# Attention decode with a key and a value cache: a quarter of each value tile weighed on GpSimd, and wider matmuls elsewhere

## The chip, the core and the metric

The kernel runs on one core of a Trainium2 chip. The time is the device time of one execution, in microseconds (us); a median over several executions is given where there are several. A profile is one further execution recorded by the hardware profiler. Its span, from the first to the last recorded instruction, is a little shorter than the device time of the same execution.

Names of engines in the profile: PE is TensorE (matmuls), PEld its weight loads, DVE is VectorE, ACT is ScalarE, POOL is GpSimd, SP is SyncE, which here issues nearly all DMAs. L252 is line 252 of the kernel.

## What is computed

One decode step of a transformer block for a batch of 4, with one query token each, in fp32. The attention reads a key and a value cache of 4 x 32 heads x 4096 positions x 128 values; these two, 268 MB each, are nearly all the bytes there are.

```python
mod = (_silu(c) @ w_mod).reshape(B, 6, 1, -1)          # c: 4x512, w_mod: 512x3072
sa, ca, ga, sb, cb, gb = (mod[:, i] for i in range(6))
h = _layernorm(x) * (1 + ca) + sa
q = (h @ wq) per head                                   # wq: 512x4096
scores = einsum("bhqd,bhkd->bhqk", q, k_cache) * Dh ** -0.5
o = einsum("bhqk,bhkd->bhqd", softmax(scores), v_cache)
x = x + ga * (o @ wo)                                   # wo: 4096x512
h = _layernorm(x) * (1 + cb) + sb
x = x + gb * (_silu(h @ w1) @ w2)                       # w1: 512x1792, w2: 1792x512
```

## The kernel before

**Tiles and slots.** The 128 pairs of batch and head are taken four heads at a time: 32 tiles, numbered n, with n = 4t + b for head group t (0 to 7) and batch b (0 to 3). A key tile k(n) and a value tile v(n) are 128 partitions x 128 rows x 128 values each, 8 MB. A partition holds 128 consecutive positions of one head. All big tiles share three slots of SBUF (`kv`, 3 buffers), given out in the order w_mod, wq, k0, v0, k1, v1, and so on to k31, v31, wo, then w1 with w2. So v(n+1) goes where k(n) was and k(n+2) goes where v(n) was: the load of v(n+1) waits for the last read of k(n), and the load of k(n+2) for the last read of v(n). SP issues the loads in this order and stands still at each wait.

**One iteration n** (loop at L353; the order on each engine is the order of the program text, since the schedule is written by hand):

- `mult` (L252): the key tile times the query, in place. GpSimd takes rows 0 to 55 (NA = 56, 7168 elements per partition) with the query from SBUF (`qw`), DVE rows 56 to 127 (9216 elements) with the query from PSUM (`qb`). `make_qb(n + 1)` prepares the next query: ACT picks a row of `qn`, a matmul spreads it over the partitions, ACT copies it to SBUF.
- `red` (L257): DVE sums each row over its 128 values into a score, first its own 72 rows, then GpSimd's 56.
- `rowmax`, `bmax`, `negmax` (L261 to L273): the maximum for the softmax, through one PE transpose. `softexp` (L279): ACT's exp. Then GpSimd writes the probabilities into two zero-padded tiles of weights, `pz` (L281, two instructions of 256 elements).
- `pv` (L297): 32 matmuls, each 4 rows of v (512 columns), accumulating in the PSUM tile `po`; the profile counts two instructions for each. Two batches share one `po` tile.
- Every second iteration `gather` (L308, L314) picks the diagonal blocks out of `po` on DVE and sums them with four matmuls. At the first batch of the next head group, `spread` (L332 to L337) scales and transposes the result for the output product.

In the last iteration (n = 31) the key tile comes in two halves, and GpSimd takes 28 of the 64 rows of each.

**Ahead and behind.** `mods` (L183) makes the six modulation vectors and L221 the queries, while the first tiles land. After the loop `project` (L346) multiplies with wo, and the feed-forward follows (L415 to L442). `busy` (L411) issues matmuls whose result nobody reads. The load of w1 and w2 is issued when the last sums over k31 are done, since it goes into k31's slot.

Of the kernel before, what the change touches and what calls it, by code (L numbers as in the profile page):

```python
# [17 lines left out]
def kernel(  # L18
# [14 lines left out]
    P = 128  # L33
# [17 lines left out]
    NA = 56  # L51
    SCALE = 1.0 / math.sqrt(Dh)
# [54 lines left out]
    tmp = s0.take(P)  # L107
    csT, hT = s0.take(NK, W), s0.take(NK, W)
# [50 lines left out]
    for t in pz:  # L159
        nc.gpsimd.memset(t, 0.0)  # L160
    oz = const.tile([P, NT, R, B], F32, name="oz")
# [15 lines left out]
    def mods(dsts, i):  # L177
        p = psum([P, 4, P], "q", 2)
        for u in range(len(dsts)):
            for k in range(NK):  # L180
                for g in range(G):
                    o = (i + u) * D + g * P
                    nc.tensor.matmul(  # L183
                        p[W * g : W * (g + 1), u, :], csT[:, k, :], wmt[:, k, o : o + P],
                        start=k == 0, stop=k == NK - 1,
                    )
        for u, d in enumerate(dsts):
            nc.scalar.activation(
                d, p[:, u, :], AF.Copy,
                scale=0.25 if i + u == 5 else 0.5, bias=1.0 if i + u in (1, 4) else 0.0,  # L190
            )
# [48 lines left out]
    def make_qb(n):  # L240
        m = work.tile([P, Dh], F32, tag="lnu", name=f"qm{n}", bufs=1)
        nc.scalar.activation(m, qn, AF.Copy, scale=sel[:, n : n + 1])  # L242
        p = psum([P, Dh], "q", 2)
        nc.tensor.matmul(p, blk.rearrange("p i x -> p (i x)"), m, start=True, stop=True)  # L244
        qb[n] = p
        qw[n] = work.tile([P, Dh], F32, tag="qw", name=f"qw{n}")
        nc.scalar.activation(qw[n], p, AF.Copy)  # L247
# [27 lines left out]
    def softexp(n):  # L275
        t, b = divmod(n, B)
        if b == 0:
            rs[t] = work.tile([P, B], F32, tag="rs", name=f"rs{t}")
        nc.scalar.activation(sc[n], sc[n], AF.Exp, bias=nm[n], accum_out=rs[t][:, b : b + 1])  # L279
        for h in range(2):  # L280
            nc.gpsimd.tensor_mul(  # L281
                pz[h][:, : HG * W].rearrange("p (g x) -> p g x", g=HG)[:, :, E:].rearrange("p g (i j) -> p g i j", i=HP),
                sc[n][:, HG * JJ * h : HG * JJ * (h + 1)].rearrange("p (g j) -> p g j", j=JJ)
                .unsqueeze(2).to_broadcast([P, HG, HP, JJ]),
                hm.unsqueeze(1).unsqueeze(3).to_broadcast([P, HG, HP, JJ]),
            )

    def pv(n):
        t, b = divmod(n, B)
        q, a = divmod(b, 2)  # L290
        if a == 0:
            po[t, q] = psum([P, JJ * Dh], "po", 2)
        for j in range(NG):
            g = j % G
            h, u = divmod(j, HG)
            o = u * W + (1 - a) * E
            nc.tensor.matmul(  # L297
                po[t, q][W * g : W * (g + 1), :],
                pz[h][:, o : o + W],
                vt[n][:, JJ * j : JJ * (j + 1), :].rearrange("p j d -> p (j d)"),  # L300
                start=(a == 0 and j < G), stop=(a == 1 and j >= NG - G),
            )
# [3 lines left out]
    def gather(t, q):  # L306
        o = work.tile([P, JJ, Dh], F32, tag="o", name="o", bufs=1)
        nc.vector.tensor_mul(  # L308
            o, po[t, q].rearrange("p (j d) -> p j d", j=JJ), jm.unsqueeze(2).to_broadcast([P, JJ, Dh])
        )  # L310
        if q == 0:
            od[t] = psum([P, Dh], "od", 1)
        for j in range(JJ):
            nc.tensor.matmul(  # L314
                od[t], spick[:, 2 - 2 * q : 2 - 2 * q + P], o[:, j, :],
                start=(q == 0 and j == 0), stop=(q == 1 and j == JJ - 1),
            )
# [21 lines left out]
    accp = psum([P, P], "acc", 1)  # L339
    nc.vector.memset(accp, 0.0)  # L340

    def project(lo, hi):
        for t in range(lo, hi):
            for r in range(R):
                for g in range(G):
                    nc.tensor.matmul(  # L346
                        accp[W * g : W * g + B, :], oz[:, t, r, :], wot[:, t, r, g * P : (g + 1) * P],
                        start=(t == 0 and r == 0), stop=(t == NT - 1 and r == R - 1),
                    )
# [3 lines left out]
    for n in range(N):  # L353
# [13 lines left out]
        if n + 1 < N:  # L367
            mult(nc.gpsimd, qw, n, 0, NA)
            mult(nc.vector, qb, n, NA, NJ)
            make_qb(n + 1)  # L370
            red(n, NA, NJ)
        else:
            for lo in (0, NJ // 2):
                mid, hi = lo + NA // 2, lo + NJ // 2
                mult(nc.gpsimd, qw, n, lo, mid)
                mult(nc.vector, qb, n, mid, hi)
                red(n, mid, hi)
            red(n, NJ // 2, NJ // 2 + NA // 2)
# [4 lines left out]
        red(n, 0, NA if n + 1 < N else NA // 2)  # L383
# [14 lines left out]
        if b == B - 1:  # L398
            norm(t)
        pv(n)  # L400
# [5 lines left out]

    idle = psum([P, P], "q", 2)
# [5 lines left out]
    x1, hg, y = (s2.take(P) for _ in range(3))  # L413
    h2T, hid, th, hidT = s2.take(NK, W), s2.take(FG), s2.take(FG), s2.take(NI, W)
    nc.vector.tensor_mul(x1, ga, accp)  # L415
    nc.vector.tensor_add(x1, x1, xg)
    busy(4)
    layernorm_mod(hg, x1, sb, cb1)
    transposed(h2T, hg, NK)
    busy(5)  # L420
# [7 lines left out]
    busy(6)  # L428
# [39 lines left out]
```

## Time and profile before

| what | before |
|---|---|
| device time, median of 3 (lowest to highest) | 1323.45 us (1323.44 to 1323.78) |
| device time of the profiled execution | 1323.81 us |
| its span | 1321.9 us |
| busy: DVE, POOL, PE, ACT | 923.3, 533.5, 398.0, 44.7 us |
| busy share of the 16 DMA engines by queue q1 | 99.4% |
| moved, mean rate | 567.76 MB, 430 GB/s |

In the profile's second part, the 40 slices of the span, the DMA row reads 9 (90% or more) in all slices but the last, which has 8. In the parts that group instructions, a row gives the line, engine, operation, output and inputs, how often, then the busy time in us and the mean of one instruction in ns, then the idle time of the engine just ahead of these instructions and what ended it. In a timeline the first number is the start, the second the duration; a bracket gives the idle time before.

### The profile page before, as it was taken

What the parts mean: (1) busy time and instruction counts of PE and PEld (TensorE: products, weight loads), DVE (VectorE), ACT (ScalarE), POOL (GpSimd) and SP (SyncE); (2) the same over time, 40 slices, a digit from 0 to 9 for tenths busy, and PEclk for the clock granted to TensorE, in tenths of its full rate; (3) what the DMA queues carried; (4) which work ended last, traced back from release to release, by engine and by line L of the source; (5) the groups of instructions that cost most, each with busy time, mean ns of one, the idle gap of its engine ahead of it and who ended that gap; (6) DMA issues with size and microseconds to landing.
All of it is one profiled execution on the core that took longest, in us unless ns stands there. A gap on an engine that the chain in (4) does not pass through costs nothing.

```text
span 1321.9 us, 7059 instructions
## 1 busy us (share of the span) xinstructions
PE 398.0 (30%) x2998; PEld 145.4 (11%) x2998; DVE 923.3 (70%) x335; ACT 44.7 (3%) x146; POOL 533.5 (40%) x111
## 2 busy tenths in 40 slices
PE   3321223323123333212333321323332132333146
PEld 2100001101010010101001010100100010010014
DVE  1267877766887666788667678776668876676971
ACT  1100000000000000000000000000000000000000
POOL 1234455433445533354543334454334445433540
PEclk9765566665566666566666656666655666665569
DMA  9999999999999999999999999999999999999998
GB/s 414 441 418 439 442 419 438 439 424 431 441 430 429 437 436 427 436 436 429 435 433 435 428 435 438 426 435 440 423 435 444 418 437 444 419 437 439 420 422 330
DMA packets 12287, 567.76 MB, mean 430 GB/s; under 512 B 1440, under 2 KB 1504, under 8 KB 2272
## 3 DMA queue, kind: packets, MB, share of 16 engines
q1 hardware_dynamic: 12048, 567.29, 99.4%
q8 instruction: 23, 0.38, 0.1%
q14 instruction: 8, 0.07, 0.0%
q0 software_dynamic: 128, 0.01, 0.0%
q10 hardware_dynamic: 80, 0.02, 0.0%
HBM read 567.30 MB, written 0.01 MB: 429 GB/s over the span
## 4 chain that ended last, share of the span: by engine, by line
DMA 32%; issue 31%; POOL 25%; PE 7%; DVE 4%; POOLq 0%; SPq 0%; DVEq 0%
DMA k<-in_A_k_cache_dram 26%; POOL k L252 24%; PE po L297 6%; DMA w<-in_B_w_dram 3%; DMA wq<-in_A_wq_dram 3%; DVE sc L257 3%; DVE k L252 1%; POOL pz L281 1%; PE q L221 1%; PE mx L231 0%; POOLq L281 0%; DVE o L308 0%; PE po L434 0%; PE mx L265 0%; SPq L123 0%
## 5 line engine op out<-in xcount | busy, mean ns | idle before, releaser
L252 POOL TENSOR_TENSOR k<-k,qw 128x7168 f32<-128x7168 f32 (+1 forms) x33 | 491.4, 14893 | 290.1 <-DMA k<-in_A_k_cache_dram 264.7
L257 DVE TENSOR_REDUCE sc<-k 128x72 f32<-128x9216 f32 (+2 forms) x66 | 554.4, 8422 | 1.1
L252 DVE TENSOR_TENSOR k<-k,q 128x9216 f32<-128x9216 f32 (+1 forms) x33 | 312.3, 9463 | 309.3 <-DMA k<-in_A_k_cache_dram 300.1
L297 PE MATMUL po<-v,pz 128*32 128x512 f32 x2048 | 292.1, 735 | 48.6 <-POOL pz L281 47.9
L281 POOL TENSOR_TENSOR pz<-sc,hm 128x256 f32<-128x256 f32 x64 | 37.9, 612 | 458.1 <-ACT sc L279 445.7
L265 PE MATMUL mx<-ident,rm 128*128 128x128 f32 x32 | 14.5, 453 | 531.2 <-DVE rm L261 531.2
L314 PE MATMUL od<-o,spick 128*128 128x128 f32 x128 | 32.3, 431 | 293.4 <-DVE o L308 293.4
L297 PEld LDWEIGHTS po<-v,pz 128*32 128x32 f32 x2048 | 71.2, 132 | 248.2 <-issue 191.9
L265 PEld LDWEIGHTS mx<-ident,rm 128*128 128x128 f32 x32 | 5.8, 181 | 538.8 <-issue 332.1
L314 PEld LDWEIGHTS od<-o,spick 128*128 128x128 f32 x128 | 27.7, 319 | 296.5 <-DVE o L308 296.3
L279 ACT ACTIVATE sc<-sc,nm 128x128 f32<-128x128 f32 x32 | 12.8, 401 | 891.9 <-DVE nm L273 891.9
L270 DVE TENSOR_REDUCE hx<-mx 128x4 f32<-128x128 f32 x32 | 9.3, 291 | 19.7 <-PE mx L265 19.7
L247 ACT ACTIVATE qw<-q 128x128 f32<-128x128 f32 x32 | 8.9, 277 | 302.9 <-PE q L244 302.9
L308 DVE TENSOR_TENSOR o<-po,jm 128x512 f32<-128x512 f32 x16 | 10.9, 680 | 8.4 <-PE po L297 8.4
L244 PE MATMUL q<-qm,blk 128*128 128x128 f32 x64 | 15.6, 326 | 1.5 <-ACT qm L242 1.5
L183 PE MATMUL q<-wm 128*32 128x128 f32 x192 | 9.2, 375 | 20.3 <-DVE wm L170 20.3
L244 PEld LDWEIGHTS q<-qm,blk 128*128 128x128 f32 x64 | 9.5, 188 | 27.0 <-issue 25.1
L242 ACT ACTIVATE qm<-qn,sel 128x128 f32<-128x128 f32 x32 | 12.4, 387 | 0.9 <-DMA xg<-in_A_x_dram 0.9
L221 PE MATMUL q<-wq,wm 128*32 128x512 f32 x64 | 9.3, 748 | 7.4 <-DMA wq<-in_A_wq_dram 7.4
L183 PEld LDWEIGHTS q<-wm 128*32 128x32 f32 x192 | 7.8, 153 | 21.0 <-DVE wm L170 20.3
L261 DVE TENSOR_REDUCE rm<-sc 128x1 f32<-128x128 f32 x32 | 9.1, 284 | 0.9
L167 DVE SCALAR_TENSOR_TENSOR wm<-wm 128x128 f32<-128x128 f32 x1 | 0.3, 291 | 12.3 <-ACT wm L166 12.3
(79 smaller groups left out, 104.2 us busy)
## 6 DMA issues: line engine op xcount, KB each, us to landing
k<-in_A_k_cache_dram SPq DMA_DIRECT2D x2, 4096.0 KB
wm<-in_w_mod_dram SPq DMA_DIRECT2D x1, 6144.0 KB
wo<-in_A_wo_dram SPq DMA_DIRECT2D x1, 4096.0 KB
wo<-in_A_wo_dram SPq DMA_DIRECT2D x1, 2048.0 KB
wo<-in_A_wo_dram SPq DMA_DIRECT2D x2, 1024.0 KB, 35.2
w<-in_B_w_dram SPq DMA_DIRECT2D x2, 1024.0 KB
w<-in_B_w_dram SPq DMA_DIRECT2D x1, 1792.0 KB
w<-in_B_w_dram SPq DMA_DIRECT2D x2, 896.0 KB
```

The costliest lines, as they stand in the source:

```text
L183: nc.tensor.matmul(p[W * g : W * (g + 1), u, :], csT[:, k, :], wmt[:, k, o : o + P], start=k == 0, stop=k == NK - 1,)
L221: nc.tensor.matmul(pq[i][W * g : W * (g + 1), :], hT[:, k, :], wqt[:, k, ch * CW : (ch + 1) * CW], start=k == 0, stop=k == NK - 1,)
L242: nc.scalar.activation(m, qn, AF.Copy, scale=sel[:, n : n + 1])
L244: nc.tensor.matmul(p, blk.rearrange("p i x -> p (i x)"), m, start=True, stop=True)
L252: eng.tensor_mul(kt[n][:, lo:hi, :], kt[n][:, lo:hi, :], src[n].unsqueeze(1).to_broadcast([P, hi - lo, Dh]))
L257: nc.vector.tensor_reduce(sc[n][:, lo:hi], kt[n][:, lo:hi, :], axis=AX.X, op=ALU.add)
L265: nc.tensor.transpose(p, nm[n].to_broadcast([P, P]), ident)
L279: nc.scalar.activation(sc[n], sc[n], AF.Exp, bias=nm[n], accum_out=rs[t][:, b : b + 1])
L281: nc.gpsimd.tensor_mul(pz[h][:, : HG * W].rearrange("p (g x) -> p g x", g=HG)[:, :, E:].rearrange("p g (i j) -> p g i j", i=HP), sc[n][:, ...
L297: nc.tensor.matmul(po[t, q][W * g : W * (g + 1), :], pz[h][:, o : o + W], vt[n][:, JJ * j : JJ * (j + 1), :].rearrange("p j d -> p (j d)") ...
L308: nc.vector.tensor_mul(o, po[t, q].rearrange("p (j d) -> p j d", j=JJ), jm.unsqueeze(2).to_broadcast([P, JJ, Dh]))
L314: nc.tensor.matmul(od[t], spick[:, 2 - 2 * q : 2 - 2 * q + P], o[:, j, :], start=(q == 0 and j == 0), stop=(q == 1 and j == JJ - 1),)
```

## The change

- **Values.** In iterations 0 to 30, rows 0 to 31 of v(n) leave the matmuls. GpSimd multiplies them in place with their probabilities (`vmult`, 4096 elements per partition) and adds rows 16 to 31 onto rows 0 to 15 (`fold`, 2048). One iteration later (`vsum(n - 1)`, behind DVE's `mult` of k(n)) DVE adds rows 8 to 15 onto 0 to 7 and 4 to 7 onto 0 to 3 (1024 and 512 elements), and one matmul with the new constant `hs` takes the four rows that are left. `pv` then has 24 matmuls, and the first `pz` tile is filled for its second half alone (128 elements).
- **Last iteration.** It keeps all 32 value matmuls; GpSimd takes 32 of each 64 rows of k31 (NL = 64), and the sums over its rows move behind DVE's own.
- **Other products.** `mods` multiplies with 512 columns of w_mod at once and picks the blocks with DVE and a second matmul. `make_qb` makes four batches with one matmul. `gather` sums its four blocks with one DVE reduction, then one matmul. `project` uses 512 columns, and its PSUM tile is summed over partition groups behind it by two copies and four matmuls.
- **Feed-forward.** One Tanh of a single column is placed ahead of the first product, and `busy` gets other counts.

```diff
+    NL = 64
+    NV = 32
...
     def make_qb(n):
-        m = work.tile([P, Dh], F32, tag="lnu", name=f"qm{n}", bufs=1)
-        nc.scalar.activation(m, qn, AF.Copy, scale=sel[:, n : n + 1])
-        p = psum([P, Dh], "q", 2)
-        nc.tensor.matmul(p, blk.rearrange("p i x -> p (i x)"), m, start=True, stop=True)
-        qb[n] = p
+        if n % B == 0:
+            m = work.tile([P, B, Dh], F32, tag="o", name=f"qm{n}", bufs=1)
+            for b in range(B):
+                nc.scalar.activation(m[:, b, :], qn, AF.Copy, scale=sel[:, n + b : n + b + 1])
+            p = psum([P, B, Dh], "q", 2)
+            nc.tensor.matmul(p, blk.rearrange("p i x -> p (i x)"), m, start=True, stop=True)
+            for b in range(B):
+                qb[n + b] = p[:, b, :]
...
+    def first(n):
+        return NV // JJ if n < N - 1 else 0
+
+    def vmult(n):
+        if first(n):
+            nc.gpsimd.tensor_mul(
+                vt[n][:, :NV, :], vt[n][:, :NV, :], sc[n][:, :NV].unsqueeze(2).to_broadcast([P, NV, Dh])
+            )
+            fold(nc.gpsimd, n, NV // 2)
+
+    def fold(eng, n, m):
+        eng.tensor_add(vt[n][:, :m, :], vt[n][:, :m, :], vt[n][:, m : 2 * m, :])
+
+    def vsum(n):
+        t, b = divmod(n, B)
+        q, a = divmod(b, 2)
+        for m in (NV // 4, JJ):
+            fold(nc.vector, n, m)
+        o = (1 - a) * E
+        nc.tensor.matmul(
+            po[t, q][0:W, :], hs[:, o : o + W], vt[n][:, :JJ, :].rearrange("p j d -> p (j d)"),
+            start=False, stop=a == 1,
+        )
...
     def gather(t, q):
...
-        for j in range(JJ):
-            nc.tensor.matmul(
-                od[t], spick[:, 2 - 2 * q : 2 - 2 * q + P], o[:, j, :],
-                start=(q == 0 and j == 0), stop=(q == 1 and j == JJ - 1),
-            )
+        s = work.tile([P, Dh], F32, tag="lnu", name="s", bufs=1)
+        nc.vector.tensor_reduce(s, o.rearrange("p j d -> p d j"), axis=AX.X, op=ALU.add)
+        nc.tensor.matmul(od[t], spick[:, 2 - 2 * q : 2 - 2 * q + P], s, start=q == 0, stop=q == 1)
...
             mult(nc.gpsimd, qw, n, 0, NA)
             mult(nc.vector, qb, n, NA, NJ)
             make_qb(n + 1)
+            if n:
+                vsum(n - 1)
             red(n, NA, NJ)
         else:
             for lo in (0, NJ // 2):
-                mid, hi = lo + NA // 2, lo + NJ // 2
+                mid, hi = lo + NL // 2, lo + NJ // 2
                 mult(nc.gpsimd, qw, n, lo, mid)
                 mult(nc.vector, qb, n, mid, hi)
+                if lo == 0:
+                    vsum(n - 1)
                 red(n, mid, hi)
...
+        vmult(n)
         pv(n)
...
+    nc.scalar.activation(th[:, 0:1], x1[:, 0:1], AF.Tanh)
```

GpSimd's order from the first to the third iteration, before. A name with a number is one buffer: k_85, k_309 and k_370 are k0, k1 and k2, sc is the score tile, L252 is `mult`, L281 fills `pz`.

```order
L252 TENSOR_TENSOR k_85<-k_85,qw_305 128x7168
L281 TENSOR_TENSOR pz_118<-sc_311,hm 128x16x16
L281 TENSOR_TENSOR pz_119<-sc_311,hm 128x16x16
L252 TENSOR_TENSOR k_309<-k_309,qw_318 128x7168
L281 TENSOR_TENSOR pz_118<-sc_372,hm 128x16x16
L281 TENSOR_TENSOR pz_119<-sc_372,hm 128x16x16
L252 TENSOR_TENSOR k_370<-k_370,qw_379 128x7168
```

The same stretch of GpSimd's order in the changed kernel, whose k0, k1 and k2 are k_85, k_261 and k_312, and whose v0 and v1 are v_259 and v_283; `mult` is L271 there, `pz` L302, the weighing L314 and the adds L320.

```order
L271 TENSOR_TENSOR k_85<-k_85,qw_257 128x7168
L302 TENSOR_TENSOR pz_118<-sc_263,hm 128x8x16
L302 TENSOR_TENSOR pz_119<-sc_263,hm 128x16x16
L314 TENSOR_TENSOR v_259<-v_259,sc_263 128x4096
L320 TENSOR_TENSOR v_259<-v_259 128x2048
L271 TENSOR_TENSOR k_261<-k_261,qw_266 128x7168
L302 TENSOR_TENSOR pz_118<-sc_314,hm 128x8x16
L302 TENSOR_TENSOR pz_119<-sc_314,hm 128x16x16
L314 TENSOR_TENSOR v_283<-v_283,sc_314 128x4096
L320 TENSOR_TENSOR v_283<-v_283 128x2048
L271 TENSOR_TENSOR k_312<-k_312,qw_317 128x7168
```

Between the second `pz` instruction of one iteration and the `mult` of the next there are now two instructions on GpSimd.

DVE's order in the third iteration (n = 2), before; k_370 is k2, `o` belongs to `gather`, rm and hx to the maximum.

```order
L252 TENSOR_TENSOR k_370<-k_370,q 128x9216
L257 TENSOR_REDUCE sc_431<-k_370 128x72
L308 TENSOR_TENSOR o<-po,jm 128x512
L257 TENSOR_REDUCE sc_431<-k_370 128x56
L261 TENSOR_REDUCE rm_449<-sc_431 128x1
```

And DVE's order in the same iteration of the changed kernel, where k_312 is k2 and v_283 is v1.

```order
L271 TENSOR_TENSOR k_312<-k_312,q 128x9216
L320 TENSOR_TENSOR v_283<-v_283 128x1024
L320 TENSOR_TENSOR v_283<-v_283 128x512
L276 TENSOR_REDUCE sc_366<-k_312 128x72
L354 TENSOR_TENSOR o<-po,jm 128x512
L360 TENSOR_REDUCE s<-o 128x128
L276 TENSOR_REDUCE sc_366<-k_312 128x56
L280 TENSOR_REDUCE rm_382<-sc_366 128x1
```

Two adds on the value tile of the iteration before now stand between DVE's `mult` and its first reduction, and in iterations with a `gather` one more reduction ahead of the second.

87 lines of the change are left out of this document (56 added, 31 removed).

## The prediction

> **What bounds the kernel now.** The page comes first: its slices and its DMA queues.
>
> ```profile
> span 1321.9 us, 7059 instructions
> DMA  9999999999999999999999999999999999999998
> q1 hardware_dynamic: 12048, 567.29, 99.4%
> ```
>
> The loads run from end to end. Windows of an eighth of an iteration say how fast; the last three columns are PE's clock, the DMA engines' busy share and GB/s.
>
> ```profile
> 377.66:382.49 4.83, 0.00 (x0) 0.00 (x0) 4.79 (x2) 0.00 (x0) 4.83 (x1) 0.50 1.00 434
> 459.77:464.60 4.83, 0.00 (x0) 0.00 (x0) 4.83 (x1) 0.00 (x0) 0.87 (x1) 0.50 0.97 421
> ```
>
> Most windows read 434, a few 421. At 434 throughout, 567.29 MB take 1307 us, so no change of the computation can win more than some 15 us. Then the waits (in total, times, longest):
>
> ```profile
> DVE k L252 <- DMA k<-in_A_k_cache_dram: 300.1, 30, 30.6
> POOL k L252 <- DMA k<-in_A_k_cache_dram: 264.7, 28, 52.8
> ```
>
> Both engines stand idle for the key tile in nearly every iteration, 8 to 10 us each time. That is the room the change has. The timeline of n = 8 to 10 shows what fills the rest: GpSimd, then DVE.
>
> ```profile
> 398.51 1.18 POOL L281 TENSOR_TENSOR pz<-sc,hm 128x256 f32<-128x256 f32 x2 [15.23 <-ACT sc L279]
> 406.59 15.37 POOL L252 TENSOR_TENSOR k<-k,qw 128x7168 f32<-128x7168 f32 x1 [6.89 <-DMA k<-in_A_k_cache_dram]
> 435.83 1.18 POOL L281 TENSOR_TENSOR pz<-sc,hm 128x256 f32<-128x256 f32 x2 [13.88 <-ACT sc L279]
> 445.29 15.35 POOL L252 TENSOR_TENSOR k<-k,qw 128x7168 f32<-128x7168 f32 x1 [8.27 <-DMA k<-in_A_k_cache_dram]
> ```
>
> ```profile
> 387.39 0.68 DVE L308 TENSOR_TENSOR o<-po,jm 128x512 f32<-128x512 f32 x1
> 387.99 7.61 DVE L257 TENSOR_REDUCE sc<-k 128x56 f32<-128x7168 f32 x1
> 395.51 0.34 DVE L332 TENSOR_SCALAR on<-od,rd 128x128 f32<-128x128 f32 x1
> 396.32 0.28 DVE L261 TENSOR_REDUCE rm<-sc 128x1 f32<-128x128 f32 x1
> 406.60 9.75 DVE L252 TENSOR_TENSOR k<-k,q 128x9216 f32<-128x9216 f32 x1 [8.69 <-DMA k<-in_A_k_cache_dram]
> 416.39 17.28 DVE L257 TENSOR_REDUCE sc<-k 128x72 f32<-128x9216 f32 x2
> 445.30 9.75 DVE L252 TENSOR_TENSOR k<-k,q 128x9216 f32<-128x9216 f32 x1 [10.07 <-DMA k<-in_A_k_cache_dram]
> ```
>
> One iteration lasts 38.7 us (406.60 to 445.30), which is two tiles of 8.39 MB at 434 GB/s. Its work is a chain: GpSimd's `mult` 15.4, DVE's reductions until 433.67 (416.39 + 17.28), 3.34 more through maximum and exp to the end of `pz` at 437.01. GpSimd is free from there to 445.29, 8.3 us. Into this gap the change puts its two instructions.
>
> **The value rows on GpSimd.** Prices come from the groups kept apart by shape (busy, mean ns):
>
> ```profile
> L252 POOL TENSOR_TENSOR k<-k,qw 128x7168 f32<-128x7168 f32 x31 | 475.8, 15350 | 290.1 <-DMA k<-in_A_k_cache_dram 264.7 <-PE po L297 16.8 <-PE q L244 8.6
> L281 POOL TENSOR_TENSOR pz<-sc,hm 128x256 f32<-128x256 f32 x64 | 37.9, 612 | 458.1 <-ACT sc L279 445.7 <-issue 12.4
> L252 POOL TENSOR_TENSOR k<-k,qw 128x3584 f32<-128x3584 f32 x2 | 15.6, 7816 | 0.0
> L160 POOL MEMSET pz<- 128x528 f32 x2 | 1.0, 537 | 0.0
> L252 DVE TENSOR_TENSOR k<-k,q 128x9216 f32<-128x9216 f32 x31 | 302.4, 9754 | 309.3 <-DMA k<-in_A_k_cache_dram 300.1 <-ACT qw L247 9.2
> L252 DVE TENSOR_TENSOR k<-k,q 128x4608 f32<-128x4608 f32 x2 | 9.9, 4949 | 0.0
> ```
>
> GpSimd takes (15350 - 612)/(7168 - 256) = 2.13 ns per element and 66 ns besides: 8.80 us for 4096 elements and 4.43 for 2048, 13.23 together. No row shows an add on GpSimd, nor a broadcast along all 128 values; the bounds are the memset's 1.0 ns per element (6.2 us) and 2.18 from the 3584 row (13.4 us). I take 13.23, since both 7168 and 256 elements, with different broadcasts, lie on that line. The Trainium skill, GPSIMD Engine Reference, section 3.1, gives 4497 ns for an add of 2048 fp32 elements on GpSimd; by it each iteration would be 0.07 us longer. The shorter first `pz` (128 elements) gives back 0.27.
>
> 13.23 does not fit into 8.3 + 0.27. GpSimd's next `mult` starts late, and everything hangs on it: DVE's reduction of its rows, the maximum, exp, `pz`, and GpSimd again. From now on this loop sets the pace, if its sum exceeds 38.7.
>
> **DVE's two adds.** At (9754 - 4949)/4608 = 1.04 ns per element and 144 ns besides, 1024 and 512 elements cost 1.8 us with a little overlap. The question is when they start. They need GpSimd's `fold`; behind it in GpSimd's queue stands `mult` of the next key tile, which waits for nothing by then, so the adds become ready just as GpSimd's longest instruction starts. The trace has one place where DVE meets a running GpSimd instruction with work that uses more than one SBUF stream, in the setup (timelines of 0.1 us around it):
>
> ```profile
> 4.56 0.54 POOL L160 MEMSET pz<- 128x528 f32 x1
> 4.59 0.61 DVE L138 TENSOR_SCALAR avg<-sel 128x32 f32<-128x32 f32 x4
> ```
>
> ```profile
> L142 DVE TENSOR_SCALAR hn<-hm 128x4 f32<-128x4 f32 x1 | 0.2, 169 | 0.0
> ```
>
> Four tiny tensor_scalars, worth 0.17 us each where GpSimd is idle (L142), start at 4.59 and are all done only at 5.20, just behind the end of GpSimd's memset at 5.10. DVE was held for the whole GpSimd instruction. DVE's `mult` is never held (9.75 us each time beside GpSimd's 15.35), but it reads the query from PSUM; the new adds read two tiles from SBUF, and no row has that beside GpSimd. The bounds are no hold and a hold of 15.35 us per iteration. I take the full hold: L138 is the nearest row, a hold that lasts as long as the GpSimd instruction. The Trainium skill, SBUF — State Buffer, section "Who interferes with whom", says that a DVE instruction with two SBUF inputs contends with a GpSimd instruction that reads SBUF, and that the second to come blocks until the first is done. By that rule the full hold stands; without it the sum is the first rival's.
>
> Behind the held adds on DVE stand both reductions and the maximum; ACT, GpSimd's `pz` and `pv` wait for those. On PE the `vsum` matmul holds the next maximum's transpose, and on SP the load of the next key tile, which comes 18 us after GpSimd's `mult` starts and, with 19.3 us of transfer, still lands while GpSimd weighs values.
>
> **The sum.** A plain iteration: 15.35 (`mult`) + 1.80 (adds) + 17.28 (both reductions, no longer beside `mult`) + 3.34 - 0.27 + 13.23 = 50.73. With a `gather` (b = 0 and 2), 0.60 (387.39 to 387.99) and as much for the new reduction: 51.93. At b = 0 `spread` adds 0.81 (395.51 to 396.32): 52.74. The start:
>
> ```profile
> 57.86 15.34 POOL L252 TENSOR_TENSOR k<-k,qw 128x7168 f32<-128x7168 f32 x1 [52.76 <-DMA k<-in_A_k_cache_dram]
> 87.11 1.18 POOL L281 TENSOR_TENSOR pz<-sc,hm 128x256 f32<-128x256 f32 x2 [13.91 <-ACT sc L279]
> ```
>
> Iteration 0 has no adds: `mult` of n = 1 starts at 88.29 - 0.27 + 13.23 = 101.3. Then n = 1 to 30: 15 x 50.73 + 8 x 51.93 + 7 x 52.74 = 1545.6, so n = 31 starts at 1646.8. There GpSimd's two halves take 17.6, the adds 1.8, and DVE has one `mult` and four reductions of 4096 elements left, 4.42 each: the last sum is at 1688.3. The end:
>
> ```profile
> 1278.96 0.28 DVE L261 TENSOR_REDUCE rm<-sc 128x1 f32<-128x128 f32 x1
> 1304.65 13.11 DMA w<-in_B_w_dram
> ```
>
> ```profile
> L346 PE MATMUL acc<-wo,oz 128*4 128x128 f32 x256 | 7.7, 273 | 2.2 <-DMA wo<-in_A_wo_dram 1.5 <-issue 0.7
> L424 PE MATMUL q<-w 128*32 128x448 f32 x32 | 3.4, 545 | 1.2 <-DMA w<-in_B_w_dram 1.1 <-DVE w L170 0.2
> L434 PE MATMUL po<-w 128*32 128x128 f32 x112 | 3.9, 276 | 2.8 <-DVE w L170 2.1 <-DMA w<-in_B_w_dram 0.7
> L166 ACT ACT_TABLE_LOAD x2 | 2.6, 1283 | 23.5 <-DMA wm<-in_c_dram 17.9 <-PE q L424 5.7
> ```
>
> From 1278.96 the kernel needs 42.9 us to its end. Without the waits for weights (1.5 + 1.1 + 0.7; wo is there long before, w1 and w2, 7.3 MB, take 17 us after the last sum) and the table load that the early Tanh moves (1.3), 38.3 remain: span 1726.6. The profiled execution took 1.9 more than its span, and lies 0.4 above the median: 1728.
>
> **Edits at nothing.** In the setup, the modulation before and the landing of wq:
>
> ```profile
> 31.10 0.79 ACT L188 ACTIVATE mod<-q 128x128 f32<-128x128 f32 x4 [5.09 <-PE q L183]
> 1.20 37.04 DMA wq<-in_A_wq_dram
> ```
>
> `mods` now passes through DVE: eight products of up to 512 elements (at most 0.68 each, L308) and as many matmuls, some 5 us in place of nothing. It ended at 31.9 and the queries wait for wq until 38.2, so it fits; if it did not, the queries and the first iteration would move by the excess, an us or two, once. `make_qb`, `gather`'s matmul, `project` and the copies behind it exchange many small PE instructions for fewer wide ones of about the same work. PE is not waited for inside the loop but for single matmuls; behind it, the same exchange is a matter of 1 us, once. `pv` with 24 of 32 matmuls frees nothing: `vsum` frees the slot, later than `pv` did.
>
> **Rivals.** *No hold.* The adds run beside `mult`, as do DVE's first reduction and `gather`. The loop is 15.35 + 7.61 + 3.07 + 13.23 = 39.26, and 40.07 at b = 0, still over 38.7. n = 31 starts at 101.3 + 30 x 39.26 + 7 x 0.81 = 1284.8, the last sum is at 1308.7, the end at 1347.0: 1349 us. For it: DVE's `mult`, undisturbed. Against: L138. If the adds get in ahead of `mult` each time, it is 30 x 1.8 = 54 us more, 1403.
>
> *The weighing is cheap.* At the memset's price the loop is 32.2 us, under 38.7, and the loads still set the end: wherever the two instructions cost under some 12.4 us and DVE isn't held, nothing moves, 1323.5. It decides at 6% below my price. For it: no row shows these forms. Against: two forms on one line. A gain would need the 421 windows to become 434, and nothing here touches them.
>
> **How the numbers follow.** Hold 0.52, no hold 0.30, cheap 0.13, something between the first two 0.05. With a hold the time is 1700 to 1765: up to 0.9 us per iteration less where the handovers overlap more than I allow, 0.17 more at 2.18 ns per element, and up to 1 us more for adds and reductions priced too low or a key tile that lands late. The range takes in the second case, down to 1340 (0.3 us less per iteration). 0.2%, 2.6 us, is what a measurement of this kernel can tell from no change. Cheap gives 0.10 for the same and 0.03 for faster; all else is slower.
>
> **What would show it.** GpSimd's `mult` should follow `fold` without a gap, and DVE's adds, 1.2 and 0.7 us of work, end 1 to 2 us after GpSimd's `mult` does; iterations of 50.7 to 52.7 us; the DMA share near three quarters. Adds that end beside a running `mult`, and iterations of 39.3, mean the first rival. GpSimd waiting for the key tile again means the second.

## The result, and the profile after

The changed kernel takes 1683.07 us (median of 6 runs, 1681.98 to 1684.64). The kernel before, beside it on the same chip, takes 1323.86 (6 runs, 1323.44 to 1324.12). The ratio is 1.2714, with a 95% interval of 1.2698 to 1.2731: 359 us are lost. The profiled execution took 1683.54, its span 1681.7. An execution more than 1.5% above the fastest of its kernel counts in no ratio here; there are two, each named at its experiment.

The page first: span, busy times, the slices of the DMA engines and the queue of the loads.

```profile
span 1681.7 us, 5475 instructions
PE 384.6 (23%) x2100; PEld 99.2 (6%) x2100; DVE 1430.6 (85%) x424; ACT 45.2 (3%) x148; POOL 883.4 (53%) x173
DMA  9987987777887777887777897777798777788765
q1 hardware_dynamic: 12048, 567.29, 79.3%
```

The same bytes are loaded as before, but the DMA engines are no longer full from end to end: 79.3% where 99.4% stood. DVE counts 507 us more as busy (1430.6 against 923.3), which is far more than two small adds need. The waits (in total, times, longest) say the same of the loads.

```profile
DVE k L271 <- DMA k<-in_A_k_cache_dram: 147.0, 31, 20.2
POOL k L271 <- DMA k<-in_A_k_cache_dram: 52.9, 1, 52.9
PE po L328 <- DVE v L320: 669.2, 31, 23.0
```

GpSimd waits for a key tile once, at the start, where it waited 28 times before. DVE still waits for one, some 4 us each time, but GpSimd starts later still. New is a long wait of PE, for DVE's adds (L320). The timeline of two iterations shows why, first on GpSimd (start, duration).

```profile
595.67 4.53 POOL L320 TENSOR_TENSOR v<-v 128x2048 f32<-128x2048 f32 x1
600.15 15.27 POOL L271 TENSOR_TENSOR k<-k,qw 128x7168 f32<-128x7168 f32 x1
636.71 0.97 POOL L302 TENSOR_TENSOR pz<-sc,hm 128x128 f32<-128x128 f32 x2 [21.29 <-ACT sc L298]
637.64 7.04 POOL L314 TENSOR_TENSOR v<-v,sc 128x4096 f32<-128x4096 f32 x1
644.75 4.53 POOL L320 TENSOR_TENSOR v<-v 128x2048 f32<-128x2048 f32 x1
649.25 15.27 POOL L271 TENSOR_TENSOR k<-k,qw 128x7168 f32<-128x7168 f32 x1
700.66 15.27 POOL L271 TENSOR_TENSOR k<-k,qw 128x7168 f32<-128x7168 f32 x1
```

And the same stretch on DVE; x2 puts both adds on one row.

```profile
590.54 9.76 DVE L271 TENSOR_TENSOR k<-k,q 128x9216 f32<-128x9216 f32 x1 [3.58 <-DMA k<-in_A_k_cache_dram]
600.23 17.00 DVE L320 TENSOR_TENSOR v<-v 128x1024 f32<-128x1024 f32 x2
617.15 17.27 DVE L276 TENSOR_REDUCE sc<-k 128x72 f32<-128x9216 f32 x2
```

GpSimd's `mult` follows `fold` at once (600.15, just as 595.67 + 4.53 ends). DVE's two adds come 0.08 us behind it and end at 617.23, 1.81 us after the `mult` does (600.15 + 15.27 = 615.42). The two reductions, the maximum, exp, `pz`, the weighing and `fold` follow one after the other, until the next `mult` at 649.25: 49.1 us for this iteration, and 51.4 for the next (649.25 to 700.66), which has a `gather` and a `spread`. The loads alone need 38.7.

That the adds end with the `mult`, and not so long after their own start, is seen where they start later. Here are a `mult` on GpSimd and the adds beside it.

```profile
749.69 15.28 POOL L271 TENSOR_TENSOR k<-k,qw 128x7168 f32<-128x7168 f32 x1
```

```profile
752.61 14.17 DVE L320 TENSOR_TENSOR v<-v 128x1024 f32<-128x1024 f32 x2
```

They start 2.9 us into the `mult`, and the pair is 2.8 us shorter than at 600.23; it ends at 766.78, again 1.81 after GpSimd (764.97). The groups kept apart by shape (busy, mean ns, idle before) give the prices.

```profile
L320 DVE TENSOR_TENSOR v<-v 128x1024 f32<-128x1024 f32 x31 | 461.4, 14885 | 13.2 <-POOL v L320 13.1
L320 DVE TENSOR_TENSOR v<-v 128x512 f32<-128x512 f32 x31 | 29.9, 965 | 1.1
L314 POOL TENSOR_TENSOR v<-v,sc 128x4096 f32<-128x4096 f32 x31 | 218.1, 7035 | 0.0
L320 POOL TENSOR_TENSOR v<-v 128x2048 f32<-128x2048 f32 x31 | 140.3, 4527 | 2.4
L360 DVE TENSOR_REDUCE s<-o 128x128 f32<-128x512 f32 x16 | 16.3, 1022 | 0.6
```

The first add (1024 elements) stands as 14.9 us of work. The second, of half its size, follows when the `mult` is over and takes 0.69 us in 30 of its 31 cases; the mean of 0.97 contains one of 9.18 us, in the last iteration, which is told at the end. The weighing took 7.04 us and not the 8.80 that the prediction had given it. `gather`'s new reduction took 1.02 and not 0.60.

### The profile page after: what moved, and what is told of

The parts are those of the page before. It is cut to its first block, busy times and chain, and to the rows that moved or that the text cites. A ratio compares the mean times of both kernels' runs of the same rounds, so it can differ in the third digit from the quotient of the medians.

```text
span 1681.7 us, 5475 instructions
## 1 busy us (share of the span) xinstructions
PE 384.6 (23%) x2100; PEld 99.2 (6%) x2100; DVE 1430.6 (85%) x424; ACT 45.2 (3%) x148; POOL 883.4 (53%) x173
## 3 DMA queue, kind: packets, MB, share of 16 engines
q1 hardware_dynamic: 12048, 567.29, 79.3%
## 4 chain that ended last, share of the span: by engine, by line
DVE 44%; DMA 26%; issue 13%; POOL 11%; PE 5%; ACT 1%; ACTq 0%; DVEq 0%; POOLq 0%; SPq 0%
DVE v L320 28%; DMA k<-in_A_k_cache_dram 25%; DVE sc L276 13%; POOL v L314 5%; POOL v L320 3%; PE po L328 2%; POOL k L271 1%; DMA wm<-in_c_dram 1%; DVE s L360 1%; POOL pz L302 1%; PE q L190 1%; PE po L343 1%; DVE o L354 0%; PE q L237 0%; PE acc L389 0%
## 5 line engine op out<-in xcount | busy, mean ns | idle before, releaser
L276 DVE TENSOR_REDUCE sc<-k 128x72 f32<-128x9216 f32 (+1 forms) x66 | 554.1, 8418 | 0.1
L271 POOL TENSOR_TENSOR k<-k,qw 128x7168 f32<-128x7168 f32 (+1 forms) x33 | 492.1, 14914 | 52.9 <-DMA k<-in_A_k_cache_dram 52.9
L320 DVE TENSOR_TENSOR v<-v 128x1024 f32<-128x1024 f32 (+1 forms) x62 | 491.4, 7925 | 14.3 <-POOL v L320 13.1
L271 DVE TENSOR_TENSOR k<-k,q 128x9216 f32<-128x9216 f32 (+1 forms) x33 | 311.2, 9431 | 147.0 <-DMA k<-in_A_k_cache_dram 147.0
L302 POOL TENSOR_TENSOR pz<-sc,hm 128x128 f32<-128x128 f32 (+1 forms) x64 | 31.2, 509 | 706.6 <-ACT sc L298 706.6
L343 PE MATMUL po<-v,pz 128*32 128x512 f32 x1552 | 242.7, 791 | 44.1 <-POOL pz L302 44.0
L314 POOL TENSOR_TENSOR v<-v,sc 128x4096 f32<-128x4096 f32 x31 | 218.1, 7035 | 0.0
L328 PE MATMUL po<-v,hs 128*32 128x512 f32 x62 | 58.4, 1046 | 669.2 <-DVE v L320 669.2
L320 POOL TENSOR_TENSOR v<-v 128x2048 f32<-128x2048 f32 x31 | 140.3, 4527 | 2.4
L343 PEld LDWEIGHTS po<-v,pz 128*32 128x32 f32 x1552 | 56.7, 140 | 208.3 <-issue 157.0
L361 PE MATMUL od<-s,spick 128*128 128x128 f32 x32 | 12.2, 484 | 140.7 <-DVE s L360 140.7
L360 DVE TENSOR_REDUCE s<-o 128x128 f32<-128x512 f32 x16 | 16.3, 1022 | 0.6
```

Of the source, the lines that this page charges most:

```text
L271: eng.tensor_mul(kt[n][:, lo:hi, :], kt[n][:, lo:hi, :], src[n].unsqueeze(1).to_broadcast([P, hi - lo, Dh]))
L276: nc.vector.tensor_reduce(sc[n][:, lo:hi], kt[n][:, lo:hi, :], axis=AX.X, op=ALU.add)
L302: nc.gpsimd.tensor_mul(pz[h][:, f * W : HG * W].rearrange("p (g x) -> p g x", g=m)[:, :, E:].rearrange("p g (i j) -> p g i j", i=HP), sc[n ...
L314: nc.gpsimd.tensor_mul(vt[n][:, :NV, :], vt[n][:, :NV, :], sc[n][:, :NV].unsqueeze(2).to_broadcast([P, NV, Dh]))
L320: eng.tensor_add(vt[n][:, :m, :], vt[n][:, :m, :], vt[n][:, m : 2 * m, :])
L328: nc.tensor.matmul(po[t, q][0:W, :], hs[:, o : o + W], vt[n][:, :JJ, :].rearrange("p j d -> p (j d)"), start=False, stop=a == 1,)
```

## The experiments

The theory behind the forecast: DVE's add has two inputs in SBUF, GpSimd's `mult` is in SBUF as well, and an add that comes while the `mult` runs is held until it ends; the length of the held stretch is GpSimd's, not the add's. Against it stood three others: that the two instructions on GpSimd are by themselves too much for the iteration (the prediction's rival without a hold, in which the adds cost next to nothing), that some other edit of the change costs the time, and that any GpSimd instruction holds the adds, whatever it does in SBUF.

**Without the adds.** DVE's adds are left out, and four matmuls with `hs` take the 16 rows that `fold` leaves. Nothing else differs from the changed kernel.

```diff
-        for m in (NV // 4, JJ):
-            fold(nc.vector, n, m)
         o = (1 - a) * E
-        nc.tensor.matmul(
-            po[t, q][0:W, :], hs[:, o : o + W], vt[n][:, :JJ, :].rearrange("p j d -> p (j d)"),
-            start=False, stop=a == 1,
-        )
+        for i in range(G):
+            nc.tensor.matmul(
+                po[t, q][0:W, :], hs[:, o : o + W], vt[n][:, JJ * i : JJ * (i + 1), :].rearrange("p j d -> p (j d)"),
+                start=False, stop=a == 1 and i == G - 1,
+            )
```

> The changed kernel without DVE's two adds: GpSimd still weighs 32 rows and folds 16 onto 16, and PE takes the 16 rows that are left with four matmuls instead of four rows with one. Theory (the adds, which read two tiles from SBUF, are held for as long as GpSimd's mult runs): with no such instruction on DVE the loop is 15.3 + 7.6 + 3.1 + 11.6 = 37.6 us, 38.4 at b = 0, which is under the 38.65 of the loads; DVE and GpSimd wait for the key tile again, and only the last iteration is some 5 us later, since GpSimd's last weighing stands ahead of its halves of k31: 1326 to 1332 us. Rival A (GpSimd's extra work alone sets the pace, the adds matter little): iterations of 39 us and more, above 1345. Rival B (the other edits cost the time): above 1600.

Measured: 1326.73 us (1326.01 to 1328.08), a ratio to the kernel before of 1.0023 (1.0013 to 1.0034). Of the 359 us that the change costs, 356 go with the two adds. Its rows show DVE waiting for the loads again, as it did before the change (300.1), GpSimd not, and the queue of the loads as full as before (99.4%):

```profile
DVE k L271 <- DMA k<-in_A_k_cache_dram: 270.1, 31, 21.5
POOL k L271 <- DMA k<-in_A_k_cache_dram: 53.1, 1, 53.1
q1 hardware_dynamic: 12048, 567.29, 99.2%
```

So the two instructions on GpSimd do fit beside the loads when nothing is held, and the rival of a GpSimd that is too slow by itself falls. They fit with nothing to spare, though: both engines had been expected to wait for the key tile again, but GpSimd waits once, at the start, where it waited 28 times before the change. The starts of its `mult` lie 38.8 us apart on average.

**The same sum with one input.** One reduction over four rows each does the work of the two adds. It reads one tile, and writes to another.

```diff
-        for m in (NV // 4, JJ):
-            fold(nc.vector, n, m)
+        s4 = work.tile([P, JJ, Dh], F32, tag="o", name=f"s4{n}", bufs=1)
+        nc.vector.tensor_reduce(
+            s4, vt[n][:, : NV // 2, :].rearrange("p (a j) d -> p j d a", j=JJ), axis=AX.X, op=ALU.add
+        )
...
-            po[t, q][0:W, :], hs[:, o : o + W], vt[n][:, :JJ, :].rearrange("p j d -> p (j d)"),
+            po[t, q][0:W, :], hs[:, o : o + W], s4.rearrange("p j d -> p (j d)"),
```

> The changed kernel with DVE's two adds replaced, at the same place and on the same 16 rows, by one tensor_reduce that has one SBUF input and does the same sum. Theory (two SBUF inputs are what is held): the reduction runs beside GpSimd's mult; at 2.0 ns per element, the price of the strided reduction in gather, it takes about 4.1 us against the adds' 15.8, and iterations are back at 38.7 us: 1328 to 1340 us. Rival C (whatever on DVE touches the rows that GpSimd has just written waits for the instruction behind the fold): the reduction too ends only behind GpSimd's mult, and the time stays above 1680.

Measured: 1334.49 us (1333.45 to 1335.40), ratio 1.0080 (1.0067 to 1.0093). In the timeline the reduction stands in the same place, behind DVE's `mult` and beside GpSimd's; first GpSimd, then DVE.

```profile
648.12 15.31 POOL L271 TENSOR_TENSOR k<-k,qw 128x7168 f32<-128x7168 f32 x1
```

```profile
649.51 3.68 DVE L326 TENSOR_REDUCE s<-v 128x512 f32<-128x2048 f32 x1
653.11 9.74 DVE L276 TENSOR_REDUCE sc<-k 128x72 f32<-128x9216 f32 x1
```

It starts 1.4 us into the `mult` and is done 3.7 us later, with 10 us of the `mult` still to come, though it reads the same rows and depends on the same `fold`. It takes 3.67 to 3.69 us in all 31 iterations. What held the adds is thus not the wait for data and not that DVE touches a value tile just then.

**All edits but the split.** `first` returns 0 throughout and `vsum` isn't called; `mods`, `make_qb`, `gather`, `project`, the last iteration's NL and the early Tanh stay as in the change.

```diff
-        return NV // JJ if n < N - 1 else 0
+        return 0
...
-            if n:
-                vsum(n - 1)
...
-                if lo == 0:
-                    vsum(n - 1)
```

> All edits but the split of the value tile: PE takes all 128 rows, GpSimd and DVE do not touch v. Theory: the loads set the end as before, and the wide products, the reduction in gather and the early Tanh lie beside them: 1322.5 to 1325 us. Rival B (the other edits cost part of the time): above 1330.

Measured: 1324.49 us (median of 12 runs; eleven lie between 1324.32 and 1324.86, one took 1355.23), ratio 1.0005 (0.9996 to 1.0014). The kernel has 6187 instructions on its engines where it had 7059, and the time is the same: the loads set it.

**The split alone.** The kernel before, with `vmult`, `fold` and `vsum` and nothing else of the change.

```diff
+        vmult(n)
         pv(n)
...
             make_qb(n + 1)
+            if n:
+                vsum(n - 1)
             red(n, NA, NJ)
```

> The kernel before with nothing but the split of the value tile. Theory: the same held adds in 30 iterations; without gather's reduction (1.02 us in 15 iterations of the held loop) it is 10 to 18 us shorter than the changed kernel: 1664 to 1676 us. Rival B: clearly less, under 1600, the rest then being the other edits.

Measured: 1665.22 us (1664.32 to 1665.56), ratio 1.2577 (1.2561 to 1.2593). The split brings 341 of the 359 us. The other 18 come from edits that cost nothing by themselves. By the starts of GpSimd's `mult`, the 15 iterations with a `gather` are 1.1 us shorter here than in the changed kernel (49.6 against 50.8 us, with a `spread` 50.3 against 51.4), 16.7 us in all, and the others are alike to 0.1 us (49.0 against 49.1). `gather`'s reduction takes 1.02 us; in a loop that the engines pace, what stands on DVE ahead of the maximum counts.

**An add that has nothing to do with the values.** To the kernel before, one add of 512 elements into a scratch tile is given to DVE behind its `mult`. In even iterations it adds two groups of DVE's own key rows, both in SBUF; in odd ones, one group and the query in PSUM.

```diff
             make_qb(n + 1)
+            u = work.tile([P, JJ, Dh], F32, tag="o", name=f"u{n}", bufs=1)
+            if n % 2 == 0:
+                nc.vector.tensor_add(u, kt[n][:, NA : NA + JJ, :], kt[n][:, NA + JJ : NA + 2 * JJ, :])
+            else:
+                nc.vector.tensor_add(u, kt[n][:, NA : NA + JJ, :], qb[n].unsqueeze(1).to_broadcast([P, JJ, Dh]))
             red(n, NA, NJ)
```

> The kernel before with one add on DVE behind its mult, 512 elements, into a scratch tile that nobody reads: in even iterations of two groups of four key rows that DVE itself has just written, in odd ones of one such group and the query in PSUM. No input or output has to do with GpSimd. Theory: in even iterations the add ends some 0.7 us behind the end of GpSimd's mult, about 6.3 us after its start; in odd ones it takes 0.7 us. The time stays within 2 us of before, since DVE has room for 6 us. Rival C (the wait comes from the rows that GpSimd has written): 0.7 us in all iterations.

The two groups, and an even iteration in the timelines of DVE and GpSimd:

```profile
L373 DVE TENSOR_TENSOR u<-k 128x512 f32<-128x512 f32 x16 | 97.7, 6108 | 0.6
L375 DVE TENSOR_TENSOR u<-k,q 128x512 f32<-128x512 f32 x15 | 10.3, 687 | 0.5
```

```profile
379.37 6.10 DVE L373 TENSOR_TENSOR u<-k 128x512 f32<-128x512 f32 x1
```

```profile
369.59 15.33 POOL L252 TENSOR_TENSOR k<-k,qw 128x7168 f32<-128x7168 f32 x1 [7.86 <-DMA k<-in_A_k_cache_dram]
```

The same number of elements takes 6.11 us with both inputs in SBUF and 0.69 with one in PSUM, while the `mult` still has 5 us to go. The slow one ends at 385.47, 0.55 us after GpSimd's `mult` (384.92), and so it does in all 16 iterations (0.54 to 0.56); it shares no data with it and waits for no one else. It writes to a tile of its own, so writing in place is not what held the adds either. GpSimd's `mult` keeps its duration (15.33). This is the hold by itself. The time of the one run was 1326.83 us, against 1323.95 of the kernel before beside it; up to 2 us had been expected, and it was 2.9; where they come from wasn't sought.

The Trainium skill, SBUF — State Buffer, section "Who interferes with whom", has it that a DVE instruction with two SBUF inputs contends with a GpSimd instruction that reads SBUF, and one with a single SBUF input, outside the modes in which DVE takes both of its port pairs, doesn't; the rows of the last runs agree (6.11 us against 0.69, and 3.68 for the reduction).

**What may hold the adds: a gap of memsets.** The same section of the Trainium skill adds that such a DVE instruction doesn't contend with a GpSimd instruction that only writes. The next kernel puts four memsets of 512 elements into GpSimd's queue between `fold` and the next `mult`, where the adds come due.

```diff
             fold(nc.gpsimd, n, NV // 2)
+            g0 = work.tile([P, JJ, Dh], F32, tag="o", name=f"g{n}", bufs=1)
+            for _ in range(4):
+                nc.gpsimd.memset(g0, 0.0)
```

> The changed kernel with four GpSimd memsets of 512 elements (2.1 us in all) into a scratch tile between the fold and the next mult. They read nothing. Theory, with the rule that two SBUF inputs are held only by a GpSimd instruction that reads SBUF: once GpSimd is late enough for DVE's mult to be done, the adds run beside the memsets, the loop is 37.6 + 2.1 = 39.7 us, and the time is 1360 to 1400 us although work was added. Rival D (any GpSimd instruction holds them, as the setup's memset held the tensor_scalars): the adds wait through the memsets and the mult behind them, 51 us per iteration, 1735 to 1755 us.

Measured: 1399.89 us (1391.37 to 1405.62), ratio 1.0580 (1.0525 to 1.0635). GpSimd, then DVE, in one iteration (in this kernel the adds are L323):

```profile
681.82 4.51 POOL L323 TENSOR_TENSOR v<-v 128x2048 f32<-128x2048 f32 x1
686.27 2.27 POOL L320 MEMSET g<- 128x512 f32 x4
688.50 15.29 POOL L271 TENSOR_TENSOR k<-k,qw 128x7168 f32<-128x7168 f32 x1
```

```profile
686.36 1.95 DVE L323 TENSOR_TENSOR v<-v 128x1024 f32<-128x1024 f32 x2 [2.19 <-POOL v L323]
```

Both adds run beside the memsets in 1.95 us, and the memsets take the 2.27 us that they also take in an iteration without adds beside them. More work on GpSimd makes the kernel 283 us faster than the change. A memset, which only writes, does not hold them, so the rival of "any GpSimd instruction" falls, by the trace and by its expected time. In the first two of these iterations the adds came due only after the `mult` had begun (DVE's own `mult`, of a late key tile, ended at 106.77, GpSimd's began at 102.32), and there they were held again, until 119.4.

**All adds on GpSimd.** DVE's two adds move to GpSimd, behind `fold`.

```diff
-        for m in (NV // 4, JJ):
-            fold(nc.vector, n, m)
...
-            fold(nc.gpsimd, n, NV // 2)
+            for m in (NV // 2, NV // 4, JJ):
+                fold(nc.gpsimd, n, m)
```

> The changed kernel with the two small adds on GpSimd too, behind its fold, none on DVE. Theory: nothing is held; 1024 and 512 elements at the measured 2.2 ns add 3.4 us to GpSimd's loop, 41.0 us, 41.8 at b = 0, over the 38.65 of the loads, so GpSimd's chain sets the pace: 1390 to 1412 us.

Measured: 1416.39 us (1415.04 to 1417.65), ratio 1.0697 (1.0681 to 1.0713), 4 us over the range expected. GpSimd's timeline:

```profile
636.92 8.28 POOL L321 TENSOR_TENSOR v<-v 128x2048 f32<-128x2048 f32 x3
645.16 15.29 POOL L271 TENSOR_TENSOR k<-k,qw 128x7168 f32<-128x7168 f32 x1
686.68 15.28 POOL L271 TENSOR_TENSOR k<-k,qw 128x7168 f32<-128x7168 f32 x1
```

The three adds take 8.28 us, and the loop 41.5 (645.16 to 686.68): too long for the loads' 38.7, but 7.6 us shorter than with the hold. On the engine where they are slow they cost less than on the one where they must wait.

**Why the weighing was cheaper than forecast.** To the kernel before, GpSimd is given one instruction of 2048 elements per iteration, of four kinds in turn: a product with a score spread along the 128 values, one with a row of 128 spread over the rows (the form of `mult`), one of two tiles, and an add of two tiles.

```diff
+        if n + 1 < N:
+            a, c = vt[n][:, :16, :], vt[n][:, 16:32, :]
+            if b == 0:
+                nc.gpsimd.tensor_mul(a, a, sc[n][:, :16].unsqueeze(2).to_broadcast([P, 16, Dh]))
+            elif b == 1:
+                nc.gpsimd.tensor_mul(a, a, qw[n].unsqueeze(1).to_broadcast([P, 16, Dh]))
+            elif b == 2:
+                nc.gpsimd.tensor_mul(a, a, c)
+            else:
+                nc.gpsimd.tensor_add(a, a, c)
         pv(n)
```

> The kernel before with one GpSimd instruction of 2048 elements on the value tile behind pz, where GpSimd is idle, by batch: b = 0 the tile times a score spread along its 128 values, b = 1 the tile times a row spread over the 16 rows (the form of mult), b = 2 a product of two tiles, b = 3 an add of two tiles. It spoils the value rows that it touches. Theory: the form with one score per 128 values costs 1.7 ns per element (3.5 us), the other three 2.13 to 2.2 (4.4 to 4.6). Rival E (products of the value tile are cheap because DVE rests at that time): all four at 3.5 to 3.7. The time stays within 2 us of before.

The four groups, in this order:

```profile
L403 POOL TENSOR_TENSOR v<-v,sc 128x2048 f32<-128x2048 f32 x8 | 28.9, 3607 | 0.0
L405 POOL TENSOR_TENSOR v<-v,qw 128x2048 f32<-128x2048 f32 x8 | 36.0, 4494 | 0.0
L407 POOL TENSOR_TENSOR v<-v 128x2048 f32<-128x2048 f32 x8 | 36.0, 4498 | 0.0
L409 POOL TENSOR_TENSOR v<-v 128x2048 f32<-128x2048 f32 x7 | 31.5, 4493 | 0.0
```

Three forms cost the same, 4.49 to 4.50 us, so rival E falls. The product with the score, which stays the same along the innermost 128 elements, costs 3.61, a fifth less. The form goes with the batch here, but the batch is not the reason: in the changed kernel the weighing takes 7.03 or 7.04 us at every batch. Between 2048 and 4096 elements it is (7035 - 3607)/2048 = 1.67 ns per element, against the 2.13 that the prediction drew from the other forms. The time did not move (1323.58 us in one run, 1323.95 before), as such an instruction fits into the iteration.

**The hold, served between pieces.** If DVE is held for one GpSimd instruction and not for a stretch of them, then a `mult` in pieces lets the adds in. GpSimd's rows 0 to 55 are taken as 0 to 3, 4 to 7 and 8 to 55.

```diff
-            mult(nc.gpsimd, qw, n, 0, NA)
+            for lo, hi in ((0, 4), (4, 8), (8, NA)):
+                mult(nc.gpsimd, qw, n, lo, hi)
             mult(nc.vector, qb, n, NA, NJ)
```

> The changed kernel with GpSimd's mult in three instructions, rows 0 to 3, 4 to 7 and 8 to 55, and nothing else. In the last iteration of the changed kernel, where mult comes in two halves, the first add ended at the boundary between them. Theory (the hold lasts for one GpSimd instruction, and DVE is served at the boundary while GpSimd then waits in its turn): once GpSimd is late enough for DVE's mult to be done, the two adds run at the first two boundaries, GpSimd's mult takes 15.3 + 0.1 + 1.8, and the loop is 39.5 us, 40.3 at b = 0; with two or three held iterations at the start 1365 to 1405 us. Rival F (instructions of GpSimd that stand back to back keep DVE out): 50 us per iteration and more, 1680 to 1700 us.

Measured: 1407.39 us (median of 4 runs, 1401.38 to 1424.79) and 1403.14 without the longest (the profiled execution took as much); ratio 1.0625 (1.0589 to 1.0661). The range expected ended at 1405: the second of these medians is inside, the first 2 us over. GpSimd's three pieces in two iterations, and DVE's adds in the first:

```profile
686.93 17.00 POOL L271 TENSOR_TENSOR k<-k,qw 128x512 f32<-128x512 f32 x3
726.40 17.01 POOL L271 TENSOR_TENSOR k<-k,qw 128x512 f32<-128x512 f32 x3
```

```profile
687.01 3.94 DVE L320 TENSOR_TENSOR v<-v 128x1024 f32<-128x1024 f32 x2
```

The pair takes 3.94 us in place of 17.00, at the price of 1.7 us on GpSimd (17.00 against 15.27), and the loop 39.5 us in place of 49.1. GpSimd's next instruction was queued and waited for nothing, and DVE was served all the same: the hold ends with the instruction that caused it. Where the adds come due later than the first piece, one of them meets the long third piece and is held for it. In the profiled execution that is so in three of the 30 iterations ahead of the last, at 106.47, 150.93 and 637.43, where the pair takes 10.84, 15.35 and 15.84 us; in the others it takes 3.94 at most.

**The best form of the split that was found.** The kernel without the adds was still 2.9 us behind. The maximum that follows its last sum:

```profile
1287.01 0.29 DVE L280 TENSOR_REDUCE rm<-sc 128x1 f32<-128x128 f32 x1
```

It starts 8 us later than in the kernel before (1278.96), since the weighing of v30 stands on GpSimd ahead of `mult` in the last iteration. In the next kernel iteration 30 isn't split either.

```diff
-        return NV // JJ if n < N - 1 else 0
+        return NV // JJ if n < N - 2 else 0
...
-                if lo == 0:
-                    vsum(n - 1)
```

> The kernel in which PE takes the sixteen rows that GpSimd's fold leaves, with the split left out in iteration 30 too. Theory: its 3 us over the kernel before came from GpSimd's last weighing, which stood ahead of the halves of k31 and put the last sum at 1287.0 instead of 1279.0; without it the last sum is back at 1279 to 1280, and the time is that of the kernel before, 1323 to 1325 us, not below it, since the loads set the end. Rival: 1326 to 1328 as with the weighing, the 3 us then being somewhere else.

Measured: 1324.17 us (1323.93 to 1324.80), ratio 1.0003 (0.9994 to 1.0012). The same row of this kernel, as early as before:

```profile
1278.03 0.29 DVE L280 TENSOR_REDUCE rm<-sc 128x1 f32<-128x128 f32 x1
```

So a quarter of 30 of the 32 value tiles can go to GpSimd at no cost, and brings nothing either, because PE was not what the kernel waited for. No version of the change here is faster than the kernel before.

## Where the prediction was right, and where not

The forecast was 1728 us, and 1683.07 was measured, 45 less. For the case with a hold the prediction gave 1700 to 1765. The time lies 17 us under that, and inside the whole range, 1340 to 1765, only because this was drawn to take in the rival without a hold. The mechanism was right, then, and the size of a term was not.

**What bounds the kernel: right.** The loads set the pace, no change of the computation could win much. Two kernels with fewer matmuls, all edits but the split and the last experiment, stand at the old time (1324.49 and 1324.17 us).

**The hold: right, and nearly the whole of the loss.** The adds were taken as held for GpSimd's `mult`, their end 1 to 2 us after it; it is 1.80 to 1.82 in all 30 iterations ahead of the last. Without the adds it is 1326.73 us, with a reduction that isn't held in their place 1334.49; so it is the hold that costs the time, and not the adds' work.

**The row that spoke for it: right in its direction, not the same thing.** The prediction took the full hold from DVE's tensor_scalars beside a memset in the setup. As printed there it doesn't show a hold, since 0.61 us for four is less than four times 0.17. Single durations do: the four take 0.35 to 0.55 us each and end between 5.14 and 5.20, right behind the memset. But the run with the memsets shows that a memset does not hold these adds at all. So there are two cases that look alike, DVE held by a GpSimd instruction, and which of them applies depends on the forms of both instructions. As far as this row goes, the right answer was luck. Why those tensor_scalars ended with the memset wasn't tried and stays open; the Trainium skill, in the same section of SBUF — State Buffer, counts tensor_scalar among the forms that can take both of DVE's port pairs, and no run here shows that.

**The price of the weighing: the step that was wrong.** "I take 13.23, since both 7168 and 256 elements, with different broadcasts, lie on that line." Weighing and `fold` took 7.04 and 4.53 us, 11.57 together. `fold` lay on the line; the weighing is a form for which the line doesn't hold (3.61 against 4.49 us for 2048 elements). An iteration is shorter by 1.66 us for that, and 30 of them by 49.8.

**`gather`'s reduction: too low.** It was priced like the product ahead of it, 0.60, and took 1.02, 15 times: 6.3 us more. It reads its 4 blocks across, with 128 elements between two that are summed; whether this distance or the short sums cost the time wasn't tried.

**The sum with these two terms.** The second `mult` on GpSimd started at 99.73, 1.6 ahead of the forecast, as the first weighing was cheaper too. The 30 iterations behind it were forecast at 1545.6 us and took 1502.1 (99.73 to 1601.81); 1545.6 - 49.8 + 6.3 = 1502.1. From there to the last sum it was 40.9 us (41.5 forecast), and the end took 39.0 (38.3). All of it: 1726.6 - 1.6 - 43.5 - 0.6 + 0.7 = 1681.6, and the span is 1681.7. It also holds kind by kind: with the two terms put right, a plain iteration comes to 49.07 us, one with a `gather` to 50.69, one with a `spread` too to 51.50, and the trace has 49.07, 50.76 and 51.42 on average. So the sum is not right by errors that cancel between the kinds.

**The threshold.** The prediction said that two instructions under some 12.4 us cost nothing if DVE isn't held. At 11.57 that came out: without the adds the kernel lost only 2.9 us, and all but 0.3 of them went when iteration 30 wasn't split. The 12.4 itself wasn't tried, and at 11.57 GpSimd had no wait for the loads left. The rival's condition on the price was met, that on the hold was not. Its chance on record, 0.13, was for both together; the case that came, a cheap weighing with a full hold, had no chance and no time of its own.

**The edits at nothing: right in the old loop.** Alone they give 1324.49 us. Beside the split they cost 18, as said above: what is hidden depends on who sets the pace.

## What to carry to other kernels

Before a two-input instruction is given to VectorE, look at what GpSimd has in its queue at the moment when the instruction comes due: if that is a long product of tiles in SBUF and the small one has both inputs in SBUF, the small one costs as much as the long one has left, whatever its own size. An input in PSUM, a reduction with one input, a matmul, or a GpSimd instruction cut so that a boundary falls where the small one comes due, each avoided it here. And a price per element holds for a form of access, not for an operation: take it from a row with the same broadcast, or keep both ends.

## What the runs showed of the hardware that had not been expected

**GpSimd has two prices for a product.** 2048 elements take 4.49 to 4.50 us, and 3.61 if one operand is a single value spread along the innermost 128 elements.

**DVE is served between two GpSimd instructions, and the second of them is longer by that.** In the last iteration of the changed kernel, GpSimd's `mult` comes in two halves of equal size, one right behind the other. GpSimd's two halves:

```profile
1601.81 8.80 POOL L271 TENSOR_TENSOR k<-k,qw 128x4096 f32<-128x4096 f32 x1
```

```profile
1610.57 9.78 POOL L271 TENSOR_TENSOR k<-k,qw 128x4096 f32<-128x4096 f32 x1
```

DVE's first add, of which 1.2 us are work, beside them:

```profile
1601.89 9.81 DVE L320 TENSOR_TENSOR v<-v 128x1024 f32<-128x1024 f32 x1 [8.89 <-POOL v L320]
```

The add is held to the end of the first half (1610.61) and runs then, until 1611.70; the second half, already begun by the profile, is 0.98 us longer than the first. That fits GpSimd waiting for DVE this time. The second add, behind the first, is held in its turn until the second half is over (1620.35): it ends at 1620.91, 9.18 us for the 0.69 that it takes in the other iterations.

**A sum of four across rows is dear on DVE.** 512 elements with 128 between those that are summed take 1.02 us, 2048 elements 3.68 with 512 between them: 2.0 and 1.8 ns per element, where the sums of 128 along a row take 9.74 us for 9216, 1.06 ns each. The distance and the length of the sums differ at once, so which of them costs is not shown.
